# A transformer block on Trainium2: the second pass's sixth f-tile pair multiplied out by rows, with seven products

## The chip, the cores and the metric

The kernel runs on one core of a Trainium2 chip. The metric is device time in microseconds for one launch. A core has a matrix engine (PE), a vector engine (DVE), a scalar engine (ACT), a general engine (POOL) and a queue engine that issues DMAs (SP). Each runs its own list of instructions in the order in which the program issues them, and the engines wait for each other through semaphores. SBUF is the working memory; matmuls write to PSUM, which has eight banks of 128 x 512 float32.

## The reference

One block for 2048 tokens, D = 512, F = 1792: a modulation by `c`, attention with 32 query heads over the last 512 cached keys of 8 heads, and a gated feed-forward layer.

```python
h = _layernorm(x) * (1 + ca) + sa
x = x + ga * _A_ref(h, k_cache, v_cache, wq, wo)      # softmax(q k / sqrt(128)) v, then @ wo
h = _layernorm(x) * (1 + cb) + sb
x = x + gb * (_gelu(h @ w_gate) * (h @ w_up)) @ w_down
```

The change touches the last product, `@ w_down`, and only for two of its 14 f-tiles of 128 and the second half of the tokens.

## The kernel before, in words

**Precision.** Every operand is held as two float16 parts, a high and a low one. A product is three matmuls: low by high, high by high, high by low (`mm3`, line 87).

**Passes and pairs.** The feed-forward layer goes over the tokens in two passes of 1024 (two blocks `qb` of 512, or eight row tiles of 128). Each pass goes over seven pairs `n` of f-tiles: 0 to 6 in the first pass, 7 to 13 in the second. A pair has two f-products, gate (m = 0) and up (m = 1), counted `q` = 0 to 27; pair 12 is q 24 and 25, pair 13 is q 26 and 27. An f-product is a 2 x 2 block product done with seven block products in place of eight (Strassen and Winograd). Their order is `ORDER` = 1, 2, 6, 7, 5, 4, 3, so a position k = 0 to 6 in a `q` is one of the products, six matmuls of 512 columns each. Some products add to a bank that is read in between (`CHAIN`, line 883: 1, 6, 7, 4 share bank a; 5 and 3 share c; 2 has b): after 1, 6 and 7 the bank's state is copied or added, and the next product goes on adding to it.

**Two ways of the down product.** For a *turned* pair (0 to 6, 7 to 11) it is again seven products, in two halves p = 0, 1, with the result's columns as partitions (`yt_tasks`, line 1770): 14 tasks of three matmuls. Its operands are four tiles of gelu times up ("11", "12", "21", "22"), of which three are split into parts as they are (`result`, line 1306), and four combinations t1 to t4, made by four subtractions on POOL (`sums_of`, line 1334, profile line 1337) and split by ACT (high, line 1321) and POOL (low, line 1325). The second pass's sum of turned pairs is complete with pair 11. It is then turned back: ACT splits it (line 1733), SP transposes it by DMA, and for each of the eight row tiles 8 to 15 POOL copies the result out (`yt_row`, line 1746; profile line 1753) and adds it to the row tile's `acc` (`whole`, line 1684; profile line 1686). These two are called copy and join here.

For a *by-rows* pair (12 and 13, `NROW` = 2) a row tile is one task of six matmuls of 512 columns, 48 matmuls for a pair (`y_tasks`, line 958). The weights are already scaled by `gb` and prepared in attention (`prep_wd`, line 1428, POOL work, stored by SP to DRAM and fetched later). DVE adds each task's bank to `acc` of its row tile (profile line 970); low halves of these pairs are DVE's (line 1325 too). After the second such addition the row tile goes out by DMA.

**Order of the work at the end.** The loop over `q` (line 1803) issues position after position. After positions 1, 2, 5 and 6 (2 and 5 in q 27) one *item* is taken from the list `nexty` (`y_next`): two tasks of a turned pair or one row task. `put_off(n, fn)` issues `fn` n positions later. So in q 26 the row tasks of pair 12 come at positions 1, 2, 5 and 6, in q 27 at 2 and 5, and the remaining two and the eight of pair 13 stand behind the last f-product, in what is called the tail. The copies of row tiles are issued at positions 6 of q 26 (tiles 8 and 9) and 0 (10, 11, 12 and 13) and 1 (14 and 15) of q 27. A join is issued when both the copy and the row tile's first addition have been issued, whichever is later (`halfway`, `joined`).

`acc` of row tiles 8 to 11 is loaded from DRAM at position 6 of q 23 into tiles of other uses, that of 12 to 15 later, when twelve parts have been turned.

## Time and profile before

| | |
|---|---|
| time, median of 3 runs | 1727.05 us (1726.94 to 1727.26) |
| profiled execution: span from the first to the last instruction | 1724.3 us |
| profiled execution: its own time | not recorded apart; its span lies 2.75 us under the median of the runs |
| PE busy, matmuls | 1705.4 us, 7961 |
| DVE, ACT, POOL busy | 1424.2, 1257.4, 1088.1 us |
| attention until | about 1332 us of the span |
| f-product q 26 | 1681.04 to about 1695.28 us |
| f-product q 27 | 1695.28 to 1706.94 us |
| tail: last 60 matmuls | from 1706.94 us |

How to read the lines shown below. A timeline row is: start in us, length in us, engine, line of the kernel, operation, output tile <- input tiles, shapes, count; in brackets the idle time just before and what ended it. A row with a count over 1 merges neighbours and its length goes from the first start to the last end. A row of stretches is: from:to, length, then for PE, PE's weight loads (PEld), DVE, ACT and POOL the busy time with the count of instructions, then the granted clock of PE as a share of full speed, the busy share of the DMA engines and GB/s. A row of a group is: line, engine, operation, output <- inputs, shapes, count | busy us, mean ns of one | idle time before them and what ended it. PE rows all have line 91 or that of another helper, so they are told apart by their tiles: `fa`, `fb`, `fc` are an f-product's banks, `ya`, `yb`, `yc` those of a turned pair, `py` that of a row task. The end of a matmul is modelled: one of 512 columns is shown as 0.38 us long however close the next one follows.

### The profile page before, as it was taken

Reading aid. Unit: us, or ns where it says so; the run is one execution under the profiler, and the core shown is the slowest. Engines: PE = TensorE matmul, PEld = TensorE weight load, DVE = VectorE, ACT = ScalarE, POOL = GpSimd, SP = SyncE. Lnnn points to the kernel's source line nnn. Section 1 sums busy time; section 2 is a strip of 40 time slices with the busy share of each in tenths; the row PEclk is TensorE's granted clock in tenths of the full one; section 3 lists DMA queues with packets and bytes.
Section 4 is the critical chain, followed back from the end, with each engine's and each line's share of the span. In section 5 each row is a group of like instructions: output and inputs, shape, how many; then the busy total and the mean of one; then the engine's idle time right before and its main releaser. Section 6 shows DMA issues by size and latency. Waiting matters only on the chain.

```text
span 1724.3 us, 26250 instructions
## 1 busy us (share of the span) xinstructions
PE 1705.4 (99%) x7961; PEld 780.0 (45%) x7961; DVE 1424.2 (83%) x2480; ACT 1257.4 (73%) x2823; POOL 1088.1 (63%) x1322
## 2 busy tenths in 40 slices
PE   7999999999999999999999999999999999999999
PEld 4344444444444444444444444444444444444444
DVE  8888888888888999888888888888896788676666
ACT  7988788888878877888778777788785354455442
POOL 3879777776788884655665755757760345735424
PEclk9999999999999999999999999999999999999999
DMA  7999999999999998999999999899997556365353
GB/s 242 222 207 214 214 217 205 226 202 227 213 217 236 201 212 181 212 211 225 216 220 222 211 227 206 198 236 212 222 232 162 164 144 195 121 165 174 99 158 102
DMA packets 693454, 343.51 MB, mean 199 GB/s; under 512 B 579136, under 2 KB 602688, under 8 KB 693312
## 3 DMA queue, kind: packets, MB, share of 16 engines
q1 hardware_dynamic: 693024, 341.30, 85.3%
q8 instruction: 63, 1.03, 0.3%
q14 instruction: 79, 0.65, 0.1%
q10 hardware_dynamic: 288, 0.52, 0.1%
HBM read 137.50 MB, written 63.70 MB: 117 GB/s over the span
## 4 chain that ended last, share of the span: by engine, by line
PE 92%; ACT 4%; DVE 2%; DMA 2%; issue 1%; SPq 0%; ACTq 0%; DVEq 0%
PE py L91 20%; PE po L91 18%; PE ps L91 17%; PE fa L91 8%; PE qa L91 8%; PE fc L91 4%; PE qc L91 4%; PE ya L91 4%; PE qb L91 2%; PE fb L91 2%; PE yc L91 2%; ACT ee L1009 1%; ACT p L1021 1%; PE yb L91 1%; DMA rw<-in_wq 1%
## 5 line engine op out<-in xcount | busy, mean ns | idle before, releaser
L1009 ACT ACTIVATE ee<-ps,nm 128x512 f32<-128x512 f32 x512 | 349.7, 683 | 185.3 <-DVE nm L1000 182.7
L1026 DVE SCALAR_TENSOR_TENSOR p<-ee,rr,p 128x512 f16<-128x512 f32 x512 | 454.4, 888 | 8.5 <-ACT p L1021 8.0
L1000 DVE TENSOR_REDUCE nm<-ps 128x1 f32<-128x512 f32 x512 | 350.1, 684 | 96.8 <-PE ps L91 94.9
L91 PE MATMUL ps<-k,qt 128*128 128x512 f16 x1536 | 414.7, 379 | 4.4 <-ACT ee L1009 3.3
L1021 ACT ACTIVATE p<-ee,rr 128x512 f16<-128x512 f32 x512 | 363.9, 711 | 16.5 <-DVE rr L1017 11.8
L91 PE MATMUL po<-pt,v 128*128 128x512 f16 x1536 | 372.9, 379 | 2.1 <-DMA pt<-p 0.8
L91 PE MATMUL py<-wo,ot 128*128 128x512 f16 x1536 | 371.3, 379 | 0.0
L91 PEld LDWEIGHTS <-w 128*128 128x128 f16 x2184 | 213.4, 98 | 259.6 <-issue 2.0
L91 PEld LDWEIGHTS <-v 128*128 128x128 f16 x1536 | 149.8, 98 | 184.6 <-issue 3.0
L91 PEld LDWEIGHTS <-ot 128*128 128x128 f16 x1536 | 150.3, 98 | 181.2
L91 PEld LDWEIGHTS <-qt 128*128 128x128 f16 x1536 | 145.7, 98 | 178.0 <-issue 6.0
L1337 POOL TENSOR_TENSOR fg<-fg 128x512 f32<-128x512 f32 x48 | 62.9, 1311 | 135.8 <-DVE fg L1311 133.0
L754 DVE SCALAR_TENSOR_TENSOR ot<-po,ot 128x512 f16<-128x512 f32 x128 | 87.8, 686 | 40.4 <-ACT ot L753 39.9
L1321 ACT ACTIVATE at<-fg 128x512 f16<-128x512 f32 x92 | 56.3, 626 | 77.8 <-DVE fg L1311 61.0
L1009 ACT ACTIVATION_READ_ACCUMULATOR ee<-ps,nm 128x1 f32 x512 | 100.1, 196 | 0.0
L970 DVE SCALAR_TENSOR_TENSOR acc<-py,ysc,acc 128x512 f32<-128x512 f32 x128 | 94.7, 739 | 5.3 <-PE py L91 5.3
L91 PE MATMUL qa<-t,w 128*128 128x512 f16 x348 | 84.9, 379 | 0.0
L91 PE MATMUL fa<-t,w 128*128 128x512 f16 x336 | 81.7, 379 | 0.1
L237 POOL TENSOR_TENSOR lw<-lw,half__86 128x1 f32<-128x1 f32 x38 | 25.9, 681 | 85.7 <-DVE lw L188 85.6
L753 ACT ACTIVATE ot<-po 128x512 f16<-128x512 f32 x128 | 73.9, 578 | 5.0 <-PE po L91 5.0
L404 POOL TENSOR_TENSOR rs<-rs,nhalf 128x1 f32<-128x1 f32 x32 | 18.5, 577 | 93.7 <-DVE rs L398 85.8
L91 PEld LDWEIGHTS <-wo 128*128 128x128 f16 x504 | 49.3, 98 | 59.7 <-issue 0.5
(258 smaller groups left out, 2802.9 us busy)
## 6 DMA issues: line engine op xcount, KB each, us to landing
w<-kept SPq DMA_DIRECT2D x123, 256.0 KB, 3.3
wo<-kept SPq DMA_DIRECT2D x72, 256.0 KB, 3.2
kept<-stage SPq DMA_DIRECT2D x67, 256.0 KB, 3.0
raw<-in_wo SPq DMA_DIRECT2D x56, 256.0 KB, 3.2
kept<-w SPq DMA_DIRECT2D x39, 256.0 KB, 3.0
rw<-in_wq SPq DMA_DIRECT2D x38, 256.0 KB, 3.1
hs<-hf SPq DMA_DIRECT2D x32, 256.0 KB, 2.9
pt<-p SPq DMA_TRANSPOSE x512, 3.4
```

The source lines that it names most:

```text
L91: nc.tensor.matmul(ps, a, b, start=first and n == 0, stop=last and n == 2, skip_group_check=chain)
L237: nc.gpsimd.tensor_tensor(out, out, half_, op=ALU.pow)
L404: nc.gpsimd.tensor_tensor(st["rs"], st["rs"], nhalf, op=ALU.pow)
L753: nc.scalar.activation(t[:, 0, :], src, AF.Copy, scale=scale)
L754: return lambda: nc.vector.scalar_tensor_tensor(t[:, 1, :], src, scale, t[:, 0, :], op0=ALU.mult, op1=ALU.subtract)
L970: nc.vector.scalar_tensor_tensor(acc[ti], st["p"], by, acc[ti], op0=ALU.mult, op1=ALU.add)
L1000: nc.vector.tensor_reduce(nm, E[t]["ps"], axis=AX.X, op=ALU.max, negate=True)
L1009: nc.scalar.activation(e, E[t]["ps"], AF.Exp, bias=E[t]["nm"], scale=1.0, accum_out=sm[:, t % 2:t % 2 + 1])
L1021: nc.scalar.activation(p16[:, 0, :], E[t]["e"], AF.Copy, scale=E[t]["r"])
L1026: nc.vector.scalar_tensor_tensor(p16[:, 1, :], E[t]["e"], E[t]["r"], p16[:, 0, :], op0=ALU.mult, op1=ALU.subtract)
L1321: nc.scalar.activation(t[:, 0, :], g, AF.Copy)
L1337: nc.gpsimd.tensor_tensor(g[o], g[a], g[b], op=ALU.subtract)
```

## The change: pair 12 by rows with seven products

- Pair 12 is now *mixed*. It keeps row tiles as the partitions of its result, but is multiplied out with seven products for each half p (row tiles 2p and 2p + 1 of both blocks). A product is six matmuls of 256 columns: two row tiles j side by side in one bank, three matmuls each. That makes 14 tasks and 84 matmuls, in items of two tasks: (1, 2), (6, 7), (5, 4), (3, 1'), (2', 6'), (7', 5'), (4', 3'), where a dash stands for the second half. They are taken at positions 2, 5 and 6 of q 26, 2 and 5 of q 27, and the last two in the tail.
- Each task ends with one DVE addition of a bank to 256 columns of two row tiles of `acc`, 14 in place of 8.
- Pair 12 gets the combinations t1 to t4 (POOL, ACT) of a turned pair, in place of the parts of "12".
- The weights of pair 12 are scaled by rows as before, and then combined as those of a turned pair, in attention: four stored tiles in place of two, and four fetched.
- `acc` of row tiles 8 to 15 lies in four tiles of two row tiles each (`PAIRS`), loaded at positions 4 and 6 of q 23.
- A join is issued as soon as the copy has been issued.

```diff
@@ -295,6 +295,10 @@
     def turned(n):
 
         return n < NP or n % NP < NP - NROW
+
+    def mixed(n):
+
+        return n == 2 * NP - NROW
 
     def by_rows(n):
 
@@ -1309,7 +1313,7 @@
             else:
                 g = G[n, key]
                 nc.vector.scalar_tensor_tensor(g, g, col("gsc", n % NP), src, op0=ALU.mult, op1=ALU.mult)
-                if not turned(n):
+                if not turned(n) and not mixed(n):
                     parts(key, G.pop((n, key)))
                 elif key != "12":
                     parts(key, g)
@@ -1425,7 +1429,7 @@
         sched(b + 9, (outs[1][1], [lambda: made(1, RAW[key][0]), keep_it(1)]), b + 12)
         sched(b + 10, (outs[2][1], [lambda: made(2, RAW[key][1]), keep_it(2)]), b + 13)
 
-    def prep_wd(n, b, rows_=False):
+    def prep_wd(n, b, rows_=False, seven=True):
         m, st = {}, {}
         outs = [staged() for _ in range(4)]
         l, r = slice(0, 256), slice(256, 512)
@@ -1461,8 +1465,11 @@
             nc.gpsimd.tensor_tensor(o, a, c, op=op)
 
         def d0():
-            times(st[0], col("dsc", n))
-            times(st[1], col("dsc", n))
+            for k in range(2):
+                if rows_:
+                    tt(st[k], st[k], m["g"], ALU.mult)
+                else:
+                    times(st[k], col("dsc", n))
             halves(out(0)[:, :, l], st[0][:, l])
             halves(out(0)[:, :, r], st[1][:, l])
 
@@ -1475,7 +1482,7 @@
             tt(st[0][:, l], st[1][:, r], st[0][:, l], ALU.subtract)
             tt(st[1][:, l], st[1][:, l], st[0][:, l], ALU.subtract)
 
-        if rows_:
+        if not seven:
             sched(b, (lambda: load(0), [lambda: stat(0), nop]), b + 7, kind="wr")
             sched(b + 1, (lambda: load(1), [lambda: stat(1), spread, nop]), b + 4, b + 9, kind="wr")
             for k in range(2):
@@ -1494,8 +1501,8 @@
         prep_set(2 * n, b)
         prep_set(2 * n + 1, b + (13 if n else 14))
         prep_wd(n, b + 21)
-    for n, b in ((NP - 2, T - 57), (NP - 1, T - 22)):
-        prep_wd(n, b, True)
+    prep_wd(NP - 2, T - 57, True)
+    prep_wd(NP - 1, T - 22, True, False)
     def wd_fetch(n, k):
         t = get_wo()
         WO["f", n, k] = fetch(("wd" if turned(n) else "wr", n % NP, k), t if k < 3 else t[:, :, 0:256])
@@ -1655,7 +1662,7 @@
         at(("f", q, k), *fns)
 
     for n in range(1, 2 * NP):
-        for k, at_ in ((0, 1), (2, 3), (1, 4), (3, 5)) if turned(n) else ((0, 0), (1, 1)):
+        for k, at_ in ((0, 1), (2, 3), (1, 4), (3, 5)) if turned(n) or mixed(n) else ((0, 0), (1, 1)):
             f_at(2 * n + 1, at_, lambda n=n, k=k: wd_fetch(n, k))
     for q in range(3, NQ):
         for k, at_ in ((0, 2), (3, 2), (1, 3), (2, 4)):
@@ -1682,14 +1689,12 @@
             step(k, fn)
 
     def whole(ti):
-        if ti in halfway and ti in joined:
+        if ti in joined:
             nc.gpsimd.tensor_tensor(acc[ti], acc[ti], joined[ti], op=ALU.add)
 
     def f_final(ti):
         assert ti in back
         halfway[ti] = halfway.get(ti, 0) + 1
-        if halfway[ti] == 1:
-            return whole(ti)
         if halfway[ti] < NROW:
             return
         assert ti in joined
@@ -1709,11 +1714,16 @@
             YT[key] = pool.tile([P, QB], F32, tag="acc", name="yt", bufs=2 * QT)
             nc.vector.tensor_scalar(YT[key], ps, by, None, op0=ALU.mult)
 
-    def rows_in(g, qb, tags):
-        for i in range(QT):
-            ti = 2 * QT * g + QT * qb + i
-            load_acc(ti, y1[ti], None, *tags[i // 2])
-            back.add(ti)
+    PAIRS = {}
+
+    def rows_in(g, qb):
+        for i in range(0, QT, 2):
+            t = PAIRS[qb, i // 2] = pool.tile([P, 2, D], F32, tag="h", name="yo", bufs=NB)
+            for k in range(2):
+                ti = 2 * QT * g + QT * qb + i + k
+                acc[ti] = t[:, k, :]
+                dma(acc[ti], y1[ti])
+                back.add(ti)
 
     def rows_of_first():
         for j in range(QT):
@@ -1723,7 +1733,8 @@
                 dma(acc[2 * j + k], y1[2 * j + k])
 
     f_at(2 * NP + 1, 3, rows_of_first)
-    f_at(2 * (2 * NP - NROW) - 1, 6, lambda: rows_in(1, 0, (("rw", NRW), ("wr", NWR))))
+    f_at(2 * (2 * NP - NROW) - 1, 4, lambda: rows_in(1, 0))
+    f_at(2 * (2 * NP - NROW) - 1, 6, lambda: rows_in(1, 1))
 
     def yt_turn(g, c, qb):
 
@@ -1740,8 +1751,6 @@
         split()
         put_off(3, turn)
         YR["n"] = YR.get("n", 0) + 1
-        if YR["n"] == 3 * QT:
-            put_off(4, lambda: rows_in(g, 1, (("acc", 2 * QT),) * 2))
 
     def yt_row(g, qb, i):
         t = YR["t", qb].rearrange("p c (h i) q -> p c q h i", h=2)
@@ -1796,6 +1805,36 @@
             tasks += [(lambda k=k, f=group: f(k), lambda k=k, f=post: f(k)) for k in YORDER[p]]
         return [tasks[k:k + 2] for k in range(0, len(tasks), 2)]
 
+    def mixed_tasks(n):
+        tasks = []
+        by = col("dysc", by_rows(n))
+        for p in range(2):
+            st = {}
+            bk = banks(st, {"a": ("acc", "ya", NACC) if p else ("qa", "ya", 1), "b": ("acc", "yb", NACC), "c": ("acc", "yc", NACC)})
+
+            def group(k, p=p, bk=bk):
+                a, b = PROD[k]
+                x, start = CHAIN[k]
+                ci, off = YCOL[a]
+                w, t = WO["f", n, ci], A[n, {"b11": "11", "b21": "21", "b22": "22"}.get(b, b)]
+                ps = bk(x)()
+                for j in range(2):
+                    sl = slice((2 * p + j) * P, (2 * p + j + 1) * P)
+                    o = ps[:, 256 * j:256 * j + 256]
+                    for i, (l, r) in enumerate(((0, 1), (0, 0), (1, 0))):
+                        nc.tensor.matmul(o, t[:, l, sl], w[:, r, off:off + 256], start=start and i + j == 0, stop=k in (2, 4, 3) and j == 1 and i == 2, skip_group_check=True)
+
+            def post(k, p=p, st=st):
+                (i, qb), = ADDS[k]
+                d = PAIRS[qb, p][:, :, 256 * i:256 * i + 256]
+                nc.vector.scalar_tensor_tensor(d, st[CHAIN[k][0]].rearrange("p (j d) -> p j d", j=2), by, d, op0=ALU.mult, op1=ALU.add)
+                if k == 3:
+                    for ti in (2 * QT + 2 * p, 2 * QT + 2 * p + 1, 3 * QT + 2 * p, 3 * QT + 2 * p + 1):
+                        f_final(ti)
+
+            tasks += [(lambda k=k, f=group: f(k), lambda k=k, f=post: f(k)) for k in ORDER]
+        return [tasks[k:k + 2] for k in range(0, len(tasks), 2)]
+
     YCOL = {"a11": (0, 0), "a12": (0, 256), "s2": (1, 0), "s3": (1, 256), "s4": (2, 0), "s1": (2, 256), "a22": (3, 0)}
 
     ctx.enter_context(tc.manual_schedule())
@@ -1808,11 +1847,11 @@
                 all_of(its[pk])
             run(("f", q, k))
             tick()
-            if n and k == 2 and m == 0 and turned(n - 1):
-                nexty += yt_tasks(n - 1)
+            if n and k == 2 and m == 0 and (turned(n - 1) or mixed(n - 1)):
+                nexty += (yt_tasks if turned(n - 1) else mixed_tasks)(n - 1)
             if k in {2: (2, 6), NQ - 1: (2, 5)}.get(q, (1, 2, 5, 6)):
                 y_next()
-        if m == 1 and not turned(n):
+        if m == 1 and not turned(n) and not mixed(n):
             for qi, (a, b) in enumerate((("11", "21"), ("12", "22"))):
                 for i in range(QT):
                     nexty.append(y_tasks((2 * (n // NP) + qi) * QT + i, [lambda n=n, a=a: A[n, a], lambda n=n, b=b: A[n, b]],
```

## The prediction

> **What bounds the kernel now.** I read the page first, then the chain of waits, then the busy time by stretches of the second pass's end, then the timelines of PE, DVE and POOL there.
>
> ```profile
> span 1724.3 us, 26250 instructions
> ...
> PE 1705.4 (99%) x7961; PEld 780.0 (45%) x7961; DVE 1424.2 (83%) x2480; ACT 1257.4 (73%) x2823; POOL 1088.1 (63%) x1322
> ...
> L91 PE MATMUL po<-pt,v 128*128 128x512 f16 x1536 | 372.9, 379 | 2.1 <-DMA pt<-p 0.8
> L91 PEld LDWEIGHTS <-at 128*128 128x128 f16 x96 | 9.4, 98 | 11.3
> ...
> 1681.00:1695.30 14.30, 14.30 (x68) 6.46 (x67) 7.50 (x11) 7.38 (x11) 5.67 (x5) 1.00 0.63 163
> 1695.30:1706.90 11.60, 11.60 (x55) 5.28 (x54) 7.73 (x10) 3.99 (x7) 10.95 (x10) 1.00 0.01 1
> ```
>
> PE is busy for 99% of the span, and in the two f-products of pair 13 (1681.00 to 1706.90 us, where pair 12 is multiplied out) for all of it. DVE has a third free there, ACT half or more. POOL is the engine to look at: 10.95 of 11.60 us in the second stretch.
>
> The timeline of PE over the same stretch, and one four-matmul group of 128 float32 columns from attention:
>
> ```profile
> 705.50 0.60 PE L514 MATMUL pln<-ident,acc 128*128 128x128 f32 x4
> ...
> 1693.99 1.46 PE L91 MATMUL py<-wo,at 128*128 128x512 f16 x6
> ...
> 1699.17 1.46 PE L91 MATMUL py<-wo,at 128*128 128x512 f16 x6
> ...
> 1704.35 1.46 PE L91 MATMUL py<-wo,at 128*128 128x512 f16 x6
> 1705.64 1.46 PE L91 MATMUL fc<-b,w 128*128 128x512 f16 x6
> 1706.94 13.11 PE L91 MATMUL py<-wo,at 128*128 128x512 f16 x60
> ```
>
> The last row is the tail: two row tasks of pair 12, eight of pair 13, six matmuls each. Its pitch is (13.11 - 0.38)/59 = 0.2158 us, with one weight load (98 ns) before each. So today the end follows from the number of matmuls alone.
>
> **The change part by part.** *Matmuls.* 48 of 512 columns go (48 x 0.2158 = 10.36 us); 84 of 256 columns come. The trace has none of 256 columns. From below their pitch is half of 0.2158 (0.108), from above that of 512 columns (0.2158): 9.1 to 18.1 us. I take 0.109, as the four matmuls at 705.50 run at (0.60 - 0.27)/3 = 0.109 with a load before each: 9.16 us, a gain of 1.2 us.
>
> *Banks.* The first half (p = 0) has products 6 and 7 side by side in one item, on the same bank. Product 7 adds to a bank that DVE still has to read for product 6. That takes 0.2 us to wake (the matmuls of 1704.35 end at 1705.64, the addition starts at 1705.84, below) and 0.75: 1.0 us, from 0 to 1.7 if another addition is ahead. Near zero together with the gain.
>
> *POOL.* This is the part that decides. For pair 12 POOL now also has the four sums and four low halves that it has for every turned pair. Rows of POOL:
>
> ```profile
> 1655.31 5.33 POOL L1337 TENSOR_TENSOR fg<-fg 128x512 f32<-128x512 f32 x4 [17.41 <-DVE fg L1311]
> 1660.61 4.50 POOL L1325 TENSOR_TENSOR at<-fg,at 128x512 f16<-128x512 f32 x4
> 1689.47 1.15 POOL L1753 COPY yr<-yv 128x1024 uint16<-128x1024 uint16 x1 [24.36 <-DMA yv<-yu]
> 1690.70 1.27 POOL L1686 TENSOR_TENSOR acc<-acc,yr 128x512 f32<-128x512 f32 x1
> 1691.92 1.15 POOL L1753 COPY yr<-yv 128x1024 uint16<-128x1024 uint16 x1
> ...
> 1699.23 5.37 POOL L1753 COPY yr<-yv 128x1024 uint16<-128x1024 uint16 x4
> 1704.56 1.72 POOL L1686 TENSOR_TENSOR acc<-acc,yr 128x512 f32<-128x512 f32 x1
> ```
>
> and of DVE:
>
> ```profile
> 1654.42 0.75 DVE L1311 SCALAR_TENSOR_TENSOR fg<-fg,gsc,u 128x512 f32<-128x512 f32 x1
> ...
> 1679.70 1.28 DVE L1325 TENSOR_TENSOR at<-fg,at 128x512 f16<-128x512 f32 x2
> 1680.90 0.68 DVE L1295 TENSOR_TENSOR u<-u,fc 128x512 f32<-128x512 f32 x1
> 1681.61 0.75 DVE L1311 SCALAR_TENSOR_TENSOR fg<-fg,gsc,u 128x512 f32<-128x512 f32 x1
> 1682.28 0.75 DVE L1707 SCALAR_TENSOR_TENSOR yt<-ya,dyc,yt 128x512 f32<-128x512 f32 x1
> ...
> 1705.84 0.75 DVE L970 SCALAR_TENSOR_TENSOR acc<-py,dysc,acc 128x512 f32<-128x512 f32 x1
> 1706.51 2.36 DVE L1325 TENSOR_TENSOR at<-fg,at 128x512 f16<-128x512 f32 x2
> 1708.79 0.67 DVE L1295 TENSOR_TENSOR u<-u,fc 128x512 f32<-128x512 f32 x1
> 1709.50 0.75 DVE L1311 SCALAR_TENSOR_TENSOR fg<-fg,gsc,u 128x512 f32<-128x512 f32 x1
> 1710.17 0.75 DVE L970 SCALAR_TENSOR_TENSOR acc<-py,dysc,acc 128x512 f32<-128x512 f32 x1
> ```
>
> In pair 11 the low halves end at 1660.61 + 4.50 = 1665.11, that is 10.69 us after DVE began the pair's last product (1654.42). Pair 12's last product begins at 1681.61, which the change doesn't touch, so its low halves end at 1692.30. The eight copies and joins of the turned pairs are issued behind them, at positions 6 of q 26 and 0 and 1 of q 27; today they begin at 1689.47. Four copy-join pairs take 1699.23 - 1689.47 = 9.76 us, 2.44 a pair. Now every join follows its copy at once, so joins are done two row tiles at a time at 1697.2, 1702.1, 1706.9 and 1711.8. Where DVE works on two SBUF operands meanwhile a join took 1.72 for 1.27; with three such DVE operations in that time (products 11 and 22, a low half) add 0 to 3 x 0.45 = 1.35; I take 0.7: 1712.5.
>
> *The new wait.* Before, a join came behind the row tile's first addition and DVE met it again only in the tail. Now an addition covers two row tiles of `acc`, and one that is issued behind a join must wait for it. In order of issue: product 4 of the first half (q 26, position 6) comes behind the joins of row tiles 8 and 9; product 3 (q 27, position 2) behind those of 12 and 13, at 1706.9; product 6 of the second half (q 27, position 5) behind those of 14 and 15, the last, at 1712.5. PE's items at these places start at 1693.99, 1699.17 and 1704.35 today, so every one of the three comes before its joins are done. DVE keeps its order: today's first tail addition had its matmuls done by 1706.94 + 1.3 and still began at 1710.17, behind two low halves, an addition and a product. So behind product 3's addition stand product 1' and what pair 13 needs, and behind these PE: 6' adds to the bank of 1', which is read at 1706.9 + 0.1 + 0.67 + 0.75 = 1708.4. PE comes to 6' at 1704.35 - 1.3 + 1.0 + 0.65 = 1704.7 and stands 3.7 us. Then 7' waits for the addition of 6', at 1712.5.
>
> *The end.* From 1712.5: 0.1 to wake; the addition of 6' (next start 0.67 later, as 1682.28 - 1681.61); two low halves 1.20 (1680.90 - 1679.70); the sum 0.71; the product of "12" 0.67; the addition of 7' 0.75: 1716.6. 4' waits for that one, since it adds to the same bank; 0.1, then 4' and 3', 12 x 0.109 = 1.3: the eight row tasks of pair 13 start at 1718.0. Today they start at 1706.94 + 12 x 0.2158 = 1709.53. That is 8.5 us later (7.8 to 9.2 by the join's bounds), and behind it nothing changes. PE's 1.2 us gain and the 1.0 us bank wait drop out of the sum, because they lie ahead of the wait.
>
> *PE's clock.* PE works 4.6 us (7 x 0.65) of the some 13 us between 1704.7 and 1718.0, a third. The stretches at the kernel's start show what that does:
>
> ```profile
> 12.00:16.00 4.00, 1.58 (x9) 0.83 (x8) 3.02 (x15) 2.44 (x7) 0.19 (x1) 1.00 1.05 395
> 16.00:20.00 4.00, 4.00 (x12) 1.26 (x11) 3.69 (x14) 3.70 (x6) 2.36 (x3) 0.57 0.34 128
> 20.00:24.00 4.00, 3.04 (x14) 1.05 (x12) 3.47 (x6) 3.06 (x6) 0.15 (x1) 1.00 1.02 299
> ```
>
> After 4 us with 1.58 busy the granted clock fell to 0.57 over the next 4 us; with 3.04 busy it held. A third busy is nearer to the first. One such stretch loses (1 - 0.57) x 4 = 1.7 us. Here it would fall on 7' to 3' and the first row tasks, all on the path: 0 to 3.4 us (two stretches), I take 1.7. The Trainium skill (TensorE: Matmul & The Clock Gate, "What's actually happening") halves the clock after at least one idle window of about 3.4 us. Read strictly, the wait at 6' would have to hold a whole window, which it seldom does, and this term would be 0: 1735.5. The row with 1.58 of 4 us busy speaks against so strict a reading.
>
> *What costs nothing.* In attention POOL has more to combine for these weights:
>
> ```profile
> 1193.31 1.27 POOL L1451 TENSOR_TENSOR wr<-wr,gs 128x512 f32<-128x512 f32 x1
> 1194.68 0.93 POOL L161 TENSOR_SCALAR stage<-wr 128x512 f16<-128x512 f32 x1
> 1195.69 1.16 POOL L162 TENSOR_TENSOR stage<-wr,stage 128x512 f16<-128x512 f32 x1
> 1196.81 1.27 POOL L1451 TENSOR_TENSOR wr<-wr,gs 128x512 f32<-128x512 f32 x1
> ...
> 1200.86 0.57 POOL L237 TENSOR_TENSOR lw<-lw,half__86 128x1 f32<-128x1 f32 x1
> ...
> 1208.04 0.70 POOL L165 TENSOR_SCALAR rw<-rw,fsc 128x512 f32<-128x512 f32 x1 [5.97 <-ACT p L1021]
> ...
> 1229.77 0.40 POOL L161 TENSOR_SCALAR stage<-wr 128x256 f16<-128x256 f32 x1
> ...
> 1233.62 3.48 POOL L1461 TENSOR_TENSOR wr<-wr 128x256 f32<-128x256 f32 x4
> ```
>
> Now 7.55 us (1193.31 to 1200.86). After: two products 2.54, three splits of 256 columns 3.85 (1229.77 to 1233.62), four sums 3.48, two splits of 512 columns 2 x 2.13: 14.1, so 6.6 more, against 5.97 us of idle time behind it. POOL is 0.6 us late at the next pair, and PE's waits for transposes in all of attention come to 0.8 us. I take 0, with 0.7 as the far end. The 384 KB more to store and to fetch, the loads of `acc` moved ahead on SP, the three more high halves on ACT (half idle) and DVE's six more additions (4 us in 26, a third idle) have room.
>
> **The sum.** 8.5 + 1.7 = +10.2 us on this execution: span 1724.3 to 1734.5. The runs' median lies 2.75 above the span; I keep that: 1737.3.
>
> **The rivals.**
> - *The joins block, the clock holds:* 1727.05 + 8.5 = 1735.5. For it: 6' and product 3 of q 27 break the wait up. Against: the row of 1.58 us.
> - *The joins don't hold the additions* (the order on `acc` lets them pass). Then the gain less the bank wait (-0.2) is left, and a wait in the tail: DVE comes to the first tail addition at 1710.17, so 4' starts near 1711.0 and not at 1706.94 - 0.2 + 1.3 = 1708.0: +2.9. Together 1729.7, not slower by what can be told. For it: POOL's row at 1704.56 waits behind copies today without harm. Against: both write the same `acc`, and DVE keeps its order.
> - *Only matmuls count:* 1727.05 - 1.2 = 1725.9. For it: PE at 99%. Against: everything from 1681 on.
> - *The clock stays low into the row tasks:* they take 10.4 us at full speed, so up to 1737.3 + 8.7 = 1746. Against: at 20 us it was back after one stretch of work.
>
> **How the numbers follow.** Forecast 0.70, clock holds 0.13, joins don't hold 0.09, only matmuls 0.03, clock stays low 0.05. The likeliest gives 1737.3, its own bounds (7.8 + 0 to 9.2 + 3.4) 1734.9 to 1739.7. A measurement here can tell 0.2% (3.5 us) from no change. Slower: 0.70 + 0.13 + 0.05 = 0.88; same 0.11 (the two small rivals, less a little); faster 0.01. From 1731.5 to 1741 leaves out the two small rivals and the last one.
>
> **What would show it.** Right: POOL's row of copies and joins runs without a gap from 1692 to 1712 or 1713; DVE idles before two additions of the new task for about 7 and 1 us with POOL's join (L1686 of before) named; PE idles some 3.7 us before the second half's product 6 and again before 7' and 4'; a clock under 1 after 1705. Each step wrong: matmuls of 256 columns not at 0.109; low halves not ended near 1692; no DVE wait on POOL, with PE whole to the end, which would make the forecast wrong; stalls in attention (1190 to 1215), which I price at 0.

## The result, and the profile after

| | before | after |
|---|---|---|
| time, median of 5 runs each | 1726.94 us (1725.69 to 1727.26) | 1736.32 us (1735.43 to 1737.02) |
| ratio | | 1.0056 (95% interval 1.0044 to 1.0068) |
| profiled execution: span | 1724.3 us | 1734.2 us |
| last stage: start of the first f-product of q 26 to start of the last matmul | 38.63 us | 47.85 us |
| from the start of the last matmul to the end of the span | 4.63 us | 4.09 us |

The change made the kernel 9.4 us slower. The forecast was 1737.3. The row of the last stage is the measure that the rest of this text uses, because the start of an execution varies: a row of PE that begins at 102.88 us in the kernel before begins between 101.95 us (e2) and 104.98 us (e5) in the kernels below, though what was edited lies behind it. The measure is called the *last stage* here. It is read from two rows of PE's timeline, which for the kernel before are its first row below and the tail's row of 13.11 us in the prediction: 1706.94 + 13.11 - 0.38 - 1681.04 = 38.63.

PE's timeline of the kernel before, one row:

```profile
1681.04 1.46 PE L91 MATMUL fa<-b,w 128*128 128x512 f16 x6
```

The page of the changed kernel, its first lines, and the stretches of the last stage:

```profile
span 1734.2 us, 26343 instructions
...
PE 1708.2 (99%) x7997; PEld 784.0 (45%) x7997; DVE 1425.6 (82%) x2485; ACT 1259.1 (73%) x2826; POOL 1104.1 (64%) x1340
...
1681.00:1695.30 14.30, 12.97 (x72) 6.91 (x71) 8.25 (x13) 8.73 (x13) 11.25 (x10) 1.00 0.60 144
1695.30:1706.90 11.60, 11.50 (x69) 6.55 (x67) 3.73 (x5) 3.04 (x5) 11.28 (x10) 1.00 0.01 1
1706.90:1717.00 10.10, 5.34 (x21) 2.71 (x21) 8.25 (x12) 1.26 (x2) 7.17 (x6) 0.69 0.00 0
```

The shares of the whole span hardly move: PE is at 99% before and after. The last row is where the time is: PE works 5.34 of 10.10 us, and its clock is granted at 0.69. In the row above it DVE works only 3.73 of 11.60 us (7.73 before), although it has more to add. POOL is busy for 11.28 of those 11.60 us.

The waits of the changed kernel from 1680 us to the end (waiting operation, what it waited for, us in total, times, longest):

```profile
DVE yo L1830 <- POOL yo L1693: 8.5, 2, 7.3
PE ya L1825 <- DVE yo L1830: 5.0, 4, 3.3
...
PE fc L91 <- DVE u L1299: 1.3, 1, 1.3
...
PE fa L91 <- ACT fg L907: 0.5, 1, 0.5
```

The timeline of POOL, which answers to the prediction's rows of L1337, L1325, L1753 and L1686:

```profile
1683.73 5.35 POOL L1341 TENSOR_TENSOR fg<-fg 128x512 f32<-128x512 f32 x4 [17.41 <-DVE fg L1315]
1689.03 4.51 POOL L1329 TENSOR_TENSOR at<-fg,at 128x512 f16<-128x512 f32 x4
1693.48 1.16 POOL L1762 COPY yr<-yv 128x1024 uint16<-128x1024 uint16 x1
...
1707.38 1.26 POOL L1693 TENSOR_TENSOR yo<-yo,yr 128x512 f32<-128x512 f32 x1
...
1712.71 1.60 POOL L1693 TENSOR_TENSOR yo<-yo,yr 128x512 f32<-128x512 f32 x1
```

The timeline of DVE:

```profile
1698.46 0.75 DVE L1830 SCALAR_TENSOR_TENSOR yo<-ya,dysc,yo 128x512 f32<-128x512 f32 x1 [1.25 <-POOL yo L1693]
...
1700.49 0.94 DVE L1315 SCALAR_TENSOR_TENSOR fg<-fg,gsc,fu 128x512 f32<-128x512 f32 x1
1708.68 0.75 DVE L1830 SCALAR_TENSOR_TENSOR yo<-yc,dysc,yo 128x512 f32<-128x512 f32 x1 [7.25 <-POOL yo L1693]
1709.34 0.74 DVE L1830 SCALAR_TENSOR_TENSOR yo<-ya,dysc,yo 128x512 f32<-128x512 f32 x1
1710.00 1.63 DVE L1329 TENSOR_TENSOR at<-fg,at 128x512 f16<-128x512 f32 x1
...
1714.43 0.73 DVE L1830 SCALAR_TENSOR_TENSOR yo<-ya,dysc,yo 128x512 f32<-128x512 f32 x1
```

And the timeline of PE:

```profile
1682.26 1.46 PE L91 MATMUL fa<-b,w 128*128 128x512 f16 x6
...
1693.64 0.82 PE L1825 MATMUL ya<-wo,at 128*128 128x256 f16 x6 [0.84 <-DVE yo L1830]
...
1710.14 0.84 PE L1825 MATMUL ya<-wo,at 128*128 128x256 f16 x6 [3.34 <-DVE yo L1830]
1712.28 2.72 PE L91 MATMUL fc<-b,w 128*128 128x512 f16 x6 [1.30 <-DVE u L1299]
1715.22 1.44 PE L1825 MATMUL ya<-wo,at 128*128 128x256 f16 x6 [0.22 <-DVE yo L1830]
1716.45 1.40 PE L1825 MATMUL yc<-wo,at 128*128 128x256 f16 x6
1718.46 0.81 PE L1825 MATMUL ya<-wo,at 128*128 128x256 f16 x6 [0.62 <-DVE yo L1830]
...
1719.97 10.52 PE L91 MATMUL py<-wo,at 128*128 128x512 f16 x48
```

These three read together, from right to left: the row tasks of pair 13 start at 1719.97 (1709.53 before), because PE stood 3.34 us ahead of product 6' (at 1710.14) and then three times more (1.30, 0.22 and 0.62 us). It stood there because DVE had just come to the addition of product 1' at 1709.34. DVE was late because it stood 7.25 us at the addition ahead of that one, product 3 of the first half, until 1708.68; and that addition waited for POOL's join that began at 1707.38 and took 1.26. The queue of POOL had no gap of its own to give: its copies and joins start at 1693.48, right behind the low halves that began at 1689.03.

The clock shows in the lengths: the f-product's six matmuls of 512 columns at 1712.28 take 2.72 us in place of 1.46, the products at 1715.22 and 1716.45 take 1.44 and 1.40 in place of 0.82. That is 2.5 us of longer rows. Whether they cost 2.5 us is a question for an experiment.

### The profile page after: what moved, and what is told of

Its sections match the earlier page's. It is cut to its first block, busy times and chain, and to the rows that moved or that the text cites. A ratio compares the mean times of both kernels' runs of the same rounds, so it can differ in the third digit from the quotient of the medians.

```text
span 1734.2 us, 26343 instructions
## 1 busy us (share of the span) xinstructions
PE 1708.2 (99%) x7997; PEld 784.0 (45%) x7997; DVE 1425.6 (82%) x2485; ACT 1259.1 (73%) x2826; POOL 1104.1 (64%) x1340
## 4 chain that ended last, share of the span: by engine, by line
PE 85%; ACT 5%; DVE 4%; POOL 2%; issue 2%; DMA 1%; ACTq 0%; POOLq 0%; DVEq 0%
PE py L91 18%; PE po L91 17%; PE ps L91 17%; PE qa L91 8%; PE fa L91 7%; PE qc L91 4%; PE fc L91 4%; PE ya L91 3%; PE qb L91 2%; PE fb L91 2%; PE yc L91 2%; ACT ee L1013 1%; ACT p L1025 1%; PE yb L91 1%; DVE p L1030 1%
## 5 line engine op out<-in xcount | busy, mean ns | idle before, releaser
L1030 DVE SCALAR_TENSOR_TENSOR p<-ee,rr,p 128x512 f16<-128x512 f32 x512 | 454.7, 888 | 10.2 <-ACT p L1025 9.7
L1341 POOL TENSOR_TENSOR fg<-fg 128x512 f32<-128x512 f32 x52 | 68.1, 1309 | 153.3 <-DVE fg L1315 150.3
L1325 ACT ACTIVATE at<-fg 128x512 f16<-128x512 f32 x95 | 58.2, 627 | 80.2 <-DVE fg L1315 63.1
L1712 DVE SCALAR_TENSOR_TENSOR yt<-ya,dyc,yt 128x512 f32<-128x512 f32 x82 | 60.3, 746 | 19.5 <-PE ya L91 19.5
```

Source lines behind the costliest of these rows:

```text
L1030: nc.vector.scalar_tensor_tensor(p16[:, 1, :], E[t]["e"], E[t]["r"], p16[:, 0, :], op0=ALU.mult, op1=ALU.subtract)
L1325: nc.scalar.activation(t[:, 0, :], g, AF.Copy)
L1341: nc.gpsimd.tensor_tensor(g[o], g[a], g[b], op=ALU.subtract)
L1712: nc.vector.scalar_tensor_tensor(YT[key], ps, by, YT[key], op0=ALU.mult, op1=ALU.add)
```

## The experiments

All changes are to the changed kernel unless another is named. "Ratio" is to the kernel before, with its 95% interval. The kernel before had medians of 1726.5 to 1727.1 us in these comparisons.

| kernel | time, us | ratio | last stage, us | against before |
|---|---|---|---|---|
| before | 1726.94 | | 38.63 | |
| changed | 1736.32 | 1.0056 (1.0044 to 1.0068) | 47.85 | +9.22 |
| e1, copies on ACT | 1736.31 | 1.0056 (1.0044 to 1.0069) | 47.19 | +8.56 |
| e2, joins later | 1733.73 | 1.0042 (1.0030 to 1.0055) | 45.94 | +7.31 |
| e3, weights only | 1727.62 | 1.0005 (0.9996 to 1.0014) | 38.63 | 0 |
| e4, last joins left out | 1735.83 | 1.0054 (1.0041 to 1.0067) | 47.39 | +8.76 |
| e5, clock kept | 1736.01 | 1.0057 (1.0044 to 1.0069) | 47.82 | +9.19 |
| e6, rebuilt | 1729.12 | 1.0017 (1.0008 to 1.0026) | 40.30 | +1.67 |
| e7, no copies, no joins | 1729.34 | 1.0016 (1.0008 to 1.0025) | 41.10 | +2.47 |
| e8, copies, no joins | 1729.68 | 1.0017 (1.0009 to 1.0026) | 41.09 | +2.46 |
| e9, e6 with joins at a later place | 1729.14 | 1.0015 (1.0006 to 1.0024) | 40.32 | +1.69 |
| e10, e6 without four joins | 1727.23 | 1.0006 (0.9997 to 1.0014) | 38.55 | -0.08 |
| e11, e6 with later copies | 1727.03 | 1.0004 (0.9995 to 1.0013) | 38.54 | -0.09 |

### e7 and e8: how much is POOL's copies and joins

```diff
 # e7
-            nc.gpsimd.tensor_copy(to, t[:, :, :, :, i])
             joined[ti] = r
-            whole(ti)
 # e8, in whole()
-        if ti in joined:
+        if False:
```

> The changed kernel without copies and joins of row tiles 8 to 15 (the output lacks the second pass's turned pairs): POOL has nothing to do behind its low halves. Theory: DVE waits for nothing of POOL and PE's wait before 6' goes; the bank wait (0.8), the tail's DVE wait (about 2.9) and attention (1.2) less 1.2 are left: 1730.3 us. Rival (DVE has too much with 14 additions whatever POOL does): 1733 or more, as in the run with the joins later.

> The changed kernel without the joins (the output lacks the second pass's turned pairs), the eight copies left as one unbroken run on POOL of about 8.8 us. With the joins later DVE's product 11 (two operands in SBUF) lasted 4.8 us, until POOL's run of copies and joins ended. Theory (DVE gets its second SBUF operand only when POOL pauses): that product lasts until the copies end, about 2 us here, 1731.5 us. Rival (it was the joins, or chance): 0.75 to 1.0 us as elsewhere, 1730.3 us.

Both come to the same last stage, 41.10 and 41.09 us. So the joins, with the wait that they bring, are 47.85 - 41.10 = 6.75 of the 9.22 us, and the copies alone cost the end nothing. DVE's product in e8 did last long, as expected (2.34 us, shown in the last section), but the end came no later: in e7 DVE has idle time of 0.41 and 1.31 us behind this product, and that took it up. The 14 additions are not too much by themselves either, since e7 has them all. What is left, 2.47, is the change without POOL's copies and joins at its end. PE's timeline of e7, its last rows:

```profile
1713.95 0.81 PE L1823 MATMUL ya<-wo,at 128*128 128x256 f16 x6 [1.66 <-DVE yo L1828]
...
1715.46 10.52 PE L91 MATMUL py<-wo,at 128*128 128x512 f16 x48
```

1.66 us is the wait of product 4' for the addition of 7', which stands behind two low halves, a sum and a product in DVE's queue. 0.84 is the bank wait of product 7, 0.5 a wait of an f-product for ACT's copy of its bank, and the matmuls give 1.2 back. These are 1.8. The other 0.7 comes from how an idle time is counted, from the modelled end of the row ahead: counted from start to start, less the matmuls' pitch, the three places lose 1.81, 1.01 and 0.64 us, and 0.21 is lost ahead of 3'. That is 3.67, and less 1.20 it gives the 2.47.

### e4: are the last joins the last link

```diff
-        if ti in joined:
+        if ti in joined and ti < NT - 2:
```

> The changed kernel without the joins of row tiles 14 and 15 (their output lacks the turned pairs' sum); their copies stay. Forecast's step (the addition of 6' waits for the last join and this sets the tail): the addition of 6' comes 0.6 to 1.6 us earlier, 1734.7 to 1735.7 us. Theory from the trace (DVE's queue, late since the wait for the joins of 12 and 13, comes to the addition of 6' no earlier than the last join ends): under 0.5 us, 1736.0 us.

Without the joins of row tiles 14 and 15 the end comes only 0.46 us earlier. DVE's timeline of e4:

```profile
1708.44 0.75 DVE L1830 SCALAR_TENSOR_TENSOR yo<-yc,dysc,yo 128x512 f32<-128x512 f32 x1 [7.26 <-POOL yo L1693]
...
1713.75 0.74 DVE L1830 SCALAR_TENSOR_TENSOR yo<-ya,dysc,yo 128x512 f32<-128x512 f32 x1
```

The 7.26 us wait is as before, and the addition of 6' (second row) begins 5.31 us behind it; in the changed kernel it is 1714.43 - 1708.68 = 5.75. DVE's own queue takes nearly all of this time, with or without the last joins. In the changed kernel the last join ended at 1712.71 + 1.60 = 1714.31, 0.1 us before DVE came to the addition. The forecast wait there never had to hold anybody.

### e5: what the clock cost

Idle matmuls on a constant are put ahead of the places where PE stands, so that the clock doesn't fall.

```diff
+    def busy(n):
+        ps = bank("qa", "fill", 1)
+        for _ in range(n):
+            nc.tensor.matmul(ps, ones.to_broadcast([P, P]), ones.to_broadcast([P, 512]), start=True, stop=True)
...
+                if p and k in (6, 7, 4):
+                    busy({6: 14, 7: 6, 4: 8}[k])
...
+            if (q, pk) == (NQ - 1, 3):
+                busy(5)
```

> The changed kernel with idle-time matmuls (a bank that nothing reads) in PE's waits: 14 of 512 columns before product 6', 5 before the last f-product, 6 before 7', 8 before 4', each run shorter than the wait seen there (3.0 of 3.3 us, 1.1 of 1.3, 1.3 of 1.6, 1.7 of 1.9 at full clock). Forecast's term (one stretch at half clock costs 1.7 us on the path): about 1734.6 us. Reading of the changed kernel's trace (the clock is at half for 6.8 us, but every matmul in it but 5' ends before DVE comes to its bank): 0.3 us, 1736.0 us. In both the granted clock stays 1 to the end.

The last stage of e5 begins 2.48 us later than that of the changed kernel, so two stretches of it answer to the one with 0.69:

```profile
1706.90:1717.00 10.10, 9.63 (x51) 4.81 (x49) 5.84 (x8) 1.26 (x2) 9.54 (x8) 1.00 0.01 2
1717.00:1726.00 9.00, 8.75 (x52) 4.88 (x50) 7.99 (x12) 0.63 (x1) 0.00 (x0) 1.00 0.05 20
```

The clock is at 1.00, and the last stage is 47.82 us against 47.85. The half clock cost the changed kernel nothing. DVE's queue set the order: where PE is slower its waits are shorter by as much. PE's own rows had shown 2.5 us of longer matmuls, and none of it was on the path. This holds for the place, not for the clock as such: in e2, below, the half clock fell on the row tasks, where DVE waits for PE, and there it did cost time.

### e3: the weights alone

The kernel before, with the weights of pair 12 combined and stored in attention as in the changed kernel, and the last stage as it was.

```diff
...
-    for n, b in ((NP - 2, T - 57), (NP - 1, T - 22)):
-        prep_wd(n, b, True)
+    prep_wd(NP - 2, T - 57, True)
+    prep_wd(NP - 1, T - 22, True, False)
```

> The kernel before with only the attention part of the change: the weights of pair 12 are scaled by rows and then combined to four stored tiles; pair 12 is multiplied out as before, by two of these tiles, so its part of the output is not the reference's. Forecast's price: 0 (0.7 at most), 1726.9 us. Theory from the trace of the changed kernel: POOL is 6.6 us longer there, later POOL work, a stage buffer's store and ACT's step behind it come 1.2 us late, and PE stands 1.2 us before a score product near 1249 us: 1728.1 us, with that wait in the profile.

The last stage is untouched (38.63). The time is 1.0005 with an interval that holds no change, so the time alone settles nothing. The trace shows more. PE's timeline of e3 at 1252 us, and that of the changed kernel with ACT's and POOL's rows ahead of it:

```profile
1252.02 0.81 PE L91 MATMUL ps<-k,qt 128*128 128x512 f16 x3 [1.08 <-ACT ee L1009]
```

```profile
1245.55 0.62 POOL L161 TENSOR_SCALAR stage<-wr 128x512 f16<-128x512 f32 x1 [3.46 <-DMA kept<-stage]
1249.11 0.63 ACT L385 ACTIVATE t<-cb 128x512 f16<-128x512 f32 x1 [2.61 <-POOL cb L592]
1250.46 0.81 PE L91 MATMUL ps<-k,qt 128*128 128x512 f16 x3 [1.05 <-ACT ee L1013]
```

The view of waits from 1100 to 1330 us names no wait of PE for ACT's `ee` in the kernel before; in the twelve kernels with the new weights it is 0.2 us (e1) to 1.6 us (e8), and in nine of them 0.9 or more. POOL is late, waits longer for a stage buffer that a DMA still empties, makes `cb` late, ACT stands 2.61 us for it, and the exponentials of attention that ACT has behind it come late to PE. In the kernel before the same two waits are 3.05 (POOL) and 1.50 (ACT). So the weights have a price of about 1 us in most traces, which is under what the times resolve.

### e1: the copies on ACT

```diff
-            nc.gpsimd.tensor_copy(to, t[:, :, :, :, i])
+            nc.scalar.activation(to, t[:, :, :, :, i], AF.Copy)
```

> The changed kernel with one edit: the eight copies of turned row tiles (1.15 us each on POOL) are done by ACT; order and joins are as in the changed kernel. Theory (the joins come too late, and DVE waits for them with everything behind it): POOL's joins start at the end of its low halves and take 8 x 1.27 us, so they end some 10 us earlier; DVE's waits on POOL (1.25 and 7.25 us) fall under 1 us in all, PE's 3.3 us before product 6' goes, and what is left is the bank wait (0.8), a DVE wait in the tail (about 2.9), 1.2 us lost in attention, less 1.2 us of matmuls: about 3.7 us above the kernel before, 1730.6 us. Rival (14 additions in place of 8 are simply too much for DVE): the same additions stay, so the time stays near 1736.

The time didn't move. POOL's timeline of e1, and its waits:

```profile
1699.68 10.45 POOL L1693 TENSOR_TENSOR yo<-yo,yr 128x512 f32<-128x512 f32 x8 [4.92 <-ACT yr L1762]
```

```profile
DVE yo L1830 <- POOL yo L1693: 6.1, 2, 3.8
...
PE fa L91 <- ACT u L907: 4.1, 1, 4.1
```

The last stage of e1 began 1.2 us later than that of the changed kernel (1683.50). Its joins run one after the other, 1.31 us each, and end at 1710.13, which is 5.4 us earlier in the stage than 1714.31. But the first starts at 1699.68, 3.7 us later in the stage than in the changed kernel (1694.72), because the copies stand behind a gelu in ACT's queue that waits for DVE. And six copies in a row keep ACT from copying an f-product's bank out, for which PE stands 4.1 us. The wait moved from one queue to another. This run says nothing against the joins as a cause, and nothing for the rival of too many additions.

### e2: the joins behind the additions again

```diff
 def whole(ti):
-        if ti in joined:
+        if ti in halfway and ti in joined:
...
+        if halfway[ti] == 1:
+            return whole(ti)
...
-        r = raw("yr")
+        r = pool.tile([P, D], F32, tag="acc", name="yr", bufs=2 * QT) if g else raw("yr")
```

> The changed kernel with the joins issued behind a row tile's last addition of pair 12, as in the kernel before, not right behind the copies (the copied row tiles then lie in other buffers, since eight must live at once). POOL has the same work. Theory (the order of join and addition decides): no DVE wait on POOL, 1730.6 us, as with the copies on ACT. Rival (POOL has too much work at the end, 10.7 us of sums and low halves more, wherever it stands): near 1736, since the amount is unchanged.

The additions of pair 12 no longer wait for POOL, and 1.9 us of the 9.2 came back. 1730.6 us was expected by the theory and near 1736 by its rival; 1733.73 is neither. Timelines of POOL, DVE and PE in e2:

```profile
1693.08 8.82 POOL L1764 COPY yr<-yv 128x1024 uint16<-128x1024 uint16 x8
1701.85 2.51 POOL L1693 TENSOR_TENSOR yo<-yo,yr 128x512 f32<-128x512 f32 x2
```

```profile
1700.09 4.81 DVE L1315 SCALAR_TENSOR_TENSOR fg<-fg,gsc,fu 128x512 f32<-128x512 f32 x1
```

```profile
1716.16 12.03 PE L91 MATMUL py<-wo,at 128*128 128x512 f16 x48
```

One product of DVE, 0.75 us elsewhere, lasts from 1700.09 to 1704.90. POOL works without a pause until 1701.85 + 2.51 = 1704.36. In the changed kernel the same product takes 0.94, where copies and joins take turns. This is the point that e6 to e11 follow up. The PE row shows a second loss: the row tasks take 12.03 us, 10.52 in the changed kernel, because PE's granted clock is 0.50 from about 1715.8 to 1719.2. DVE waits for PE there (1.84 us ahead of its first addition), so these 1.5 us are on the path.

### e6, e9, e10, e11: can the loss be taken back

e6 puts together what the first runs asked for: joins behind the additions (e2), copies on ACT (e1) with places further apart, the order of products of a turned pair, and items at four places of q 27 in place of two, so that nothing of pair 12 is left for the tail.

```diff
...
-            tasks += [(lambda k=k, f=group: f(k), lambda k=k, f=post: f(k)) for k in ORDER]
+            tasks += [(lambda k=k, f=group: f(k), lambda k=k, f=post: f(k)) for k in YORDER[p]]
...
-            if k in {2: (2, 6), NQ - 1: (2, 5)}.get(q, (1, 2, 5, 6)):
+            if k in {2: (2, 6), NQ - 1: (1, 2, 4, 5)}.get(q, (1, 2, 5, 6)):
...
-                            d = (7 if k == 4 else 8) + r // 2 if g else 6 + r // 2 if k == 4 else (9, 10, 10, 11)[r]
+                            d = ((7, 8, 11, 12) if k == 4 else (9, 10, 13, 14))[r] if g else 6 + r // 2 if k == 4 else (9, 10, 10, 11)[r]
```

> The changed kernel with its waits taken out: joins behind a row tile's last addition of pair 12; copies by ACT, one a position from q 26 position 6 to q 27 position 6; products 6 and 5 side by side in the first half in place of 6 and 7; four items in q 27 (positions 1, 2, 4, 5), so that none is left in the tail. Theory (the 84 shorter matmuls gain 1.2 us, attention loses 1.2, all else were waits): 1726 to 1728 us. Rival (six more additions and the combinations are too much for DVE and ACT beside pair 13): DVE's queue runs late again, 1729.5 us or more.

The time, 1729.12 us, lies between the two that were expected. The last stage falls to 40.30, and one long wait is left. Timelines of POOL, DVE and PE in e6:

```profile
1710.03 4.61 POOL L1693 TENSOR_TENSOR yo<-yo,yr 128x512 f32<-128x512 f32 x3 [3.51 <-ACT at L1325]
```

```profile
1710.47 3.04 DVE L1329 TENSOR_TENSOR at<-fg,at 128x512 f16<-128x512 f32 x2
```

```profile
1710.58 1.24 PE L91 MATMUL py<-wo,at 128*128 128x512 f16 x5
1713.57 9.46 PE L91 MATMUL py<-wo,at 128*128 128x512 f16 x43 [1.75 <-DVE at L1329]
```

PE waits 1.75 us for low halves, and two of these take 3.04 us while POOL runs three joins. Three runs, with edits to e6, ask whether the joins are the cause. In e9 four joins are issued two places later, in e10 they are left out, and in e11 nothing is left out, but the copies that they need come later in ACT's queue.

```diff
 # e9, in f_final(), and the copy no longer calls whole(ti) for these tiles
-            return whole(ti)
+            return put_off(2 if ti % QT > 1 else 0, lambda: whole(ti))
 # e10, in whole()
-        if ti in halfway and ti in joined:
+        if ti in halfway and ti in joined and ti % QT < 2:
 # e11
-                            d = ((7, 8, 11, 12) if k == 4 else (9, 10, 13, 14))[r] if g else 6 + r // 2 if k == 4 else (9, 10, 10, 11)[r]
+                            d = ((7, 8, 13, 13) if k == 4 else (9, 10, 15, 16))[r] if g else 6 + r // 2 if k == 4 else (9, 10, 10, 11)[r]
```

> The rebuilt version (joins later, copies on ACT, the first half's row tiles in an order that lets every join be ready) with the joins of row tiles 10, 11, 14 and 15 put two positions later, into the row task, so that POOL's run of joins doesn't stand in front of the low halves of pair 13. Theory (the 1.75 us that PE waits ahead of the second half of the first row task comes from POOL's joins locking DVE out of its low halves, two of which took 3.04 us): this wait goes, the last matmul starts 38.6 to 39.0 us after the first f-product of the last stage (rebuilt 40.3, before 38.63), time about 1727 (1726 to 1728), no measurable difference from before. Rival (another wait takes its place: the later joins now hold back the additions of row tiles 10 to 15): the end stays 1.5 us or more late, time 1729 or more.

> The rebuilt version without the joins of row tiles 10, 11, 14 and 15 (so these rows of the result lack the turned pairs' sum; their copies stay). Putting the joins at a later place of the program did not move them in time, since POOL runs a join as soon as its operands are there; so here they are left out. Theory (POOL's run of three joins from 1710.0 locks DVE out of the two low halves, 3.04 us in place of 1.2 to 1.3, and PE waits 1.75 us for them): the two low halves take 1.2 to 1.5 us, PE's wait ahead of the second half of the first row task goes or falls under 0.2, the last matmul starts 38.5 to 38.9 us after the first f-product of the last stage (rebuilt 40.3, before 38.63), time about 1727.4. Rival (the wait is for the product that these low halves are made of, or for something ahead of it): the low halves' end and PE's wait stay within 0.3 us of the rebuilt version's, 40.0 or more.

> The rebuilt version with ACT's copies of row tiles 10 and 11 put behind the high halves at 1709.3 us (copies about 1709.9 and 1711.1, joins not before 1711.1 and 1712.3), those of 14 and 15 behind the last high half (copies about 1715.9 and 1717.0), so that the joins really come later. Nothing is left out. Theory (the joins lock DVE out): the first of the two low halves is free, the second may meet the join of row tile 10; PE's wait falls from 1.75 to between 0 and 0.7 us, the last matmul starts 38.6 to 39.4 us after the first f-product of the last stage, time about 1727.7 (1726.5 to 1728.5), no measurable difference from before. Rival (not the joins): 40.0 or more, as the rebuilt version.

e9 missed, since its edit moved nothing in time. POOL's timeline of e9:

```profile
1710.12 4.62 POOL L1693 TENSOR_TENSOR yo<-yo,yr 128x512 f32<-128x512 f32 x3 [3.51 <-ACT at L1325]
```

The last stage of e9 began 0.07 us later than that of e6, so the three joins stand at the same place. POOL has nothing else to do there, and runs a join as soon as its operands are there, wherever in the program it is issued. DVE's timeline of e10, and POOL's, DVE's and PE's of e11:

```profile
1710.98 1.28 DVE L1329 TENSOR_TENSOR at<-fg,at 128x512 f16<-128x512 f32 x2
```

```profile
1711.35 3.52 POOL L1693 TENSOR_TENSOR yo<-yo,yr 128x512 f32<-128x512 f32 x2 [4.53 <-ACT yr L1764]
```

```profile
1710.78 1.28 DVE L1329 TENSOR_TENSOR at<-fg,at 128x512 f16<-128x512 f32 x2
```

```profile
1710.89 10.69 PE L91 MATMUL py<-wo,at 128*128 128x512 f16 x48
```

With the joins gone, or begun 0.6 us behind the first low half, the two low halves take 1.28 us in place of 3.04, and PE's 48 row matmuls run without the break. The last stage is 38.54 us, 0.09 shorter than before the change. In time e11 can't be told from the kernel before (1.0004, 0.9995 to 1.0013). So the whole loss of the changed kernel's end can be taken back by the order of the products and of POOL's and ACT's work, but the 1.2 us of fewer matmul columns does not come out as a gain: counted from start to start, 0.6 goes to the f-product's wait for ACT's copy, and the rest to three gaps of 0.1 to 0.2 us. None of these versions beats the kernel before.

## Why the prediction was right

It named the place, the engine and the direction; its sum was +10.2 us on the profiled execution, and 9.9 came: 9.22 in the last stage, 1.2 ahead of it, -0.54 behind it. Its terms were off by -1.7 (clock), +1.2 (attention), +0.7 (joins) and -0.5 (behind the last matmul), which nearly cancel. The large term was worked out; that the sum came within 0.3 us is luck. The time was 1.0 under the forecast because the median lay 2.1 us above the profiled span this time, where 2.75 was added.

- **Matmuls of 256 columns at 0.109.** Right: six are shown as 0.82 us, and (0.82 - 0.273)/5 = 0.109.
- **Bank wait of product 7, 1.0 us.** 0.84. As forecast it is not in the sum, since PE waits anyway later.
- **Low halves ended near 1692.30.** Right. Copies start at 1693.48; the last stage began 1.22 later than before, so that is 1692.26 on the prediction's scale.
- **Copies and joins at 2.44 us a pair, last join 1712.5.** Nearly: six pairs took 1693.48 to 1708.64, 2.53 a pair, and the last join ended at 1714.31 (1713.1 on that scale). The half-way price for DVE's competing operations was too low; the end lies inside the bounds given.
- **Three new waits.** Two of them are there, 1.25 and 7.25 us (about 1 and 7 were forecast). The third, of the addition of 6' for the last joins, is not: DVE got there as late through its own queue (e4).
- **PE stands 3.7 us ahead of 6', then at 7' and 4'.** 3.34, 0.22 and 0.62. A wait of 1.30 us ahead of the last f-product, behind DVE's sum, was not forecast.
- **Row tasks 8.5 us later (7.8 to 9.2).** 9.22, at the upper bound. The cause was right, late joins that hold DVE and, behind DVE, PE; the term was 0.7 short. The joins' lateness is about 0.6 of that. The last step was not as forecast: it reached the end through DVE's queue behind the second wait, not through the third wait. Both paths come to the addition of 6' within 0.1 us here, and that is luck too.
- **Clock, 1.7 us (0 to 3.4).** The step failed. The clock did fall (0.69 over 10.1 us), but the loss lay on PE, which was not the engine that set the order. e5 measures 0.03; where the half clock did fall on the row tasks, in e2, it cost 1.5. The full clock was back before the row tasks began: from 1718 us on it is 1.00 again. The prediction argued "all on the path" from PE's places in the program; it should have asked who is waited for there, and the answer stood in its own list for the end, which is a chain of DVE instructions. Its rival "the joins block, the clock holds" has the right price for a wrong reason.
- **Attention, 0 (far end 0.7).** The step failed, too low. The waits show about 1 us (1.05 in the changed kernel, 1.08 in e3), by another way than the one looked at: not PE's transposes, but a stage buffer, POOL's `cb` and ACT's exponentials. Of the 1.22 us by which the last stage began later, 0.12 is there already at PE's row of 103 us (103.00 for 102.88), and 1.10 comes behind it, so the wait is nearly all of it. In the other eleven kernels with the new weights the way from that row to the last stage is 0.6 us (e1) to 2.2 us (e8) longer than before, which is not all put down to that wait.
- **Without the joins' hold: +2.9 from a tail wait, less 0.2.** e7 and e8 come nearest to that rival: +2.47, with 1.66 of tail wait where 2.9 was worked out, and 1729.34 and 1729.68 us where 1729.7 was forecast. That the times agree is luck, since they hold attention's 1 us and the other small waits, which the rival left out.

Of the 0.54 us between the last matmul and the end, all but 0.07 lie behind DVE's last addition, in the DMA of the output: the span ends 3.4 us after it before, 2.9 in the changed kernel, and 3.1 in e3, which has the old end. The cause is open.

## What to carry to other kernels

An addition that is merged over two tiles takes over the latest of what either tile waits for: list, for every engine's queue, what now stands ahead of it, and read the price at the engine that is waited for. A slow clock on an engine that waits cost nothing here (e5), and 1.5 us where the others waited for that engine (e2); add idle work to it and see if the end moves, before charging its longer rows to the sum. In e9 the engine was idle, and an instruction's place in the program didn't set its time; to have it later, e11 made what it needs later.

## What was not expected of the hardware

**A run of POOL instructions shut DVE out for longer than one of them, but not always.** A DVE product with two operands in SBUF takes 0.75 us with POOL idle (e7) and 0.94 in the changed kernel, where POOL's copies and joins take turns. In e2 it took 4.81 us and ended 0.54 after POOL's run did (1704.90 and 1704.36); in e8 it met the end of a run of eight copies. DVE's and POOL's timelines of e8:

```profile
1701.13 2.34 DVE L1315 SCALAR_TENSOR_TENSOR fg<-fg,gsc,fu 128x512 f32<-128x512 f32 x1
```

```profile
1694.11 8.81 POOL L1762 COPY yr<-yv 128x1024 uint16<-128x1024 uint16 x8
```

It began at 1701.13 and ended at 1703.47, 0.55 us after the copies (1702.92). e6 against e10 and e11 is the test that joins are what holds low halves: the same two take 3.04 us under three joins, 1.28 without them and 1.28 when the joins start later. The prediction had bounded this by 0.45 us for each meeting, from a join that took 1.72 for 1.27. The Trainium skill (SBUF — State Buffer, "🔬 SBUF: two separate sides") has the two engines share a pair of ports under an exclusive lock, for a VectorE operation with two SBUF inputs against a GpSimd operation that reads SBUF, where the loser blocks for the whole instruction. The runs agree with the lock, but in e2 the time lost goes beyond one instruction: the product that began at 1700.09 waited out the rest of one copy, another copy and two joins. In e6 it does not go so far. An earlier low half there, and the run of four joins that it met:

```profile
1703.58 1.80 DVE L1329 TENSOR_TENSOR at<-fg,at 128x512 f16<-128x512 f32 x1
```

```profile
1701.11 5.41 POOL L1693 TENSOR_TENSOR yo<-yo,yr 128x512 f32<-128x512 f32 x4 [7.50 <-ACT yr L1764]
```

It began as the third join did and ended at 1705.38, 1.1 us before the run's end (1706.52), so it waited for about one join. What lets DVE in between two instructions of POOL in one case and not in the other is not shown.

**The clock fell without 3.4 us empty of work.** The Trainium skill (TensorE: Matmul & The Clock Gate, "What's actually happening") gives a window of about 3.4 us and the half clock after at least one idle window. Here PE stood for 3.34 us; the product behind it, at 1710.14, still ran at full speed (0.84), and the f-product at 1712.28 at half (2.72 us for 1.46). The fall, at about 1710.8 us, came after some 0.7 us of work, so the window that ended there was hardly one without any work. e2 goes further: the clock fell at about 1715.8 us though no wait of PE was longer than 1.78 us, and of the 3.40 us ahead of the fall PE was busy for 1.58. In e7, where PE is busy for 1.70 to 1.79 of 3.40 us around its wait of 1.66 us, the clock stayed at 1.00. So the work that such a window held was 0.7 us in one case and 1.6 us in the other. The half clock lasted some 6.8 us here and 3.4 us in e2, which agrees with a window of that length. The ends of matmuls are modelled, so a few tenths are open, and where the limit lies isn't shown.
